# Three seven-product stretches of a fused attention and MLP kernel: fewer second products inside each set, and attention steps 17 to 23 taken one at a time

## The chip, the cores and the metric

The kernel runs on one core of a Trainium2 chip. The core has a matrix engine (TensorE, "PE" in the profile), a vector engine (VectorE, "DVE"), an activation engine (ScalarE, "ACT"), a general engine (GpSimd, "POOL") and a sync engine (SyncE, "SP") that here only issues DMA transfers. Each engine works through its own queue of instructions, and they wait for one another by semaphores. The metric is device time in microseconds (us), the median of several runs. Matrix products are written to PSUM, which this kernel uses as eight banks of 128 x 512 float32 values.

## The reference

Decayed causal linear attention, then a two-layer MLP with a tanh GELU.

```python
for b in range(nb):                      # blocks of 64 positions, for 4 batches x 8 heads, D = 64
    intra = (qb @ kb.T * Dmask) @ vb     # Dmask = lam ** (i - j) for i >= j, else 0
    inter = (qb * lam ** (i + 1)) @ kv_state
    out[b] = intra + inter
    kv_state = lam ** 64 * kv_state + (kb * lam ** (63 - j)).T @ vb
x = out as (3072 tokens, 512)
h = x @ w_in                             # 512 -> 2048
g = gelu_tanh(h)
result = g @ w_out                       # 2048 -> 512, float32, 3072 x 512
```

## The kernel before, in words

**Attention steps.** There are 24 steps: 4 batches x 3 blocks of 256 positions x 2 halves of the heads. A step `n` is made of: `prep` (`cast_q` on DVE L282, `cast_k` on ACT L295, `scale_v` on POOL L266, and for late steps a transposing DMA on SP, L303, that makes `qkT`), `scores` (16 small PE matmuls into two banks `S`, L350), `causal` (two DVE multiplies by the mask, L360, which make `PT` and free the `S` banks), the key-value products `K` and the outputs `O` of a step (PE), and `update` (DVE `t`, L503/L506, then POOL `u`, L513: the state that a later step's inter-block matmul reads). `x_out` (ACT L487) copies `O` to the MLP's input `xT`. `R(n, s)` does the scores and `K` of step n and the `O` of step s in one go with two `S` and two `OK` banks; `burst(ns, ss)` does several steps at once with up to eight banks: two `S` for each new step, two `O` and two `K`.

**MLP groups.** The twelve 256-token blocks are taken in seven groups, `groups = [[0, 1], [2], [3], [4, 5], [6, 7], [8, 9], [10, 11]]`. Groups 1 to 6 use a seven-product scheme (Winograd's form of Strassen) for the second layer, groups 4 to 6 also for the first. For a group of 512 tokens:

- `product(m, p, part)` is half (part 0 or 1) of one second-layer product: 4 matmuls of 128x128 by 128x256. The text calls one such half P. Products 1, 2, 5, 6, 3, 7, 4 follow in this order, each for p = 0 and 1, so a group has 28 halves. They accumulate in the banks `MX` (two), `MW` and `MY`. Evacuations: ACT L657 for m = 1, 5, 6, 7, 4; DVE L677 at the end of m = 2; DVE L683 at the end of m = 3.
- `sum_g` (DVE L610, out `gs`) makes the sums of GELU values that products 5, 6, 3 and 7 read, for tiles 0 to 3 and 4 to 7 separately. `sum_x` (DVE L718, out `xs`) makes four sums of `xT`; `sum_win` (DVE L151, out `ws`) makes the weight sums of the first layer.
- `seven(m, k)` is one first-layer product of set k (k = 0 to 3): also 4 matmuls of the same shape. The text calls it S(m, k). It accumulates in the banks `HX` (one for even and one for odd sets), `HY` and `HW`. Products 1, 6, 7 and 4 of a set use the same `HX` bank in turn: DVE copies U2 out after product 6 (L763), product 7 adds to the bank, DVE makes a sum of it (L770), and only then may product 4 add to it. Product 5 of the next set overwrites `HY`, so it must come after DVE's sum of product 3 (L770). GELU is ACT L767; ACT L778 and L761 are copies.

**The order.** It is written by hand. `queue_group(g, lead, per_set)` puts the pieces of a group in a list `filler`; `fill(n)` issues the next n pieces. `merge` (L798) makes a mixed stretch: it issues the four `sum_x` behind one piece, then a lead of second products left over from the group before, then the four sets of the new group's first layer with leftover P between them, as `SLOTS[per_set]` says:

```python
for m in (1, 5, 2, 6, 3, 7):
    filler.append(lambda m=m, k=k: seven(m, k))
    if m == 5 and k > 0:
        filler.append(lambda k=k: seven(4, k - 1))
    ...
    h(slots[m])          # so many leftover P after this product
```

Everything is pinned: each engine runs its instructions in the order of the program. A call such as `prep(20)` between two `fill` calls puts a DVE, an ACT and a POOL instruction, a transposing DMA and three loads on SP at that place of each queue. The tail of the program, L1093 to L1141, is what the change rewrites. It holds three mixed stretches: group 4 with the second products of group 3, group 5 with those of group 4, group 6 with those of group 5. All banks come from one pool of eight (`ps_M`).

Of the kernel before, what the change touches and what calls it, by code (L numbers as in the profile page):

```python
# [15 lines left out]
def kernel(  # L16
# [43 lines left out]
    def load_step(s, names="qkv"):  # L60
        b, r = divmod(s, 2 * NSB)
        sb, half = divmod(r, 2)
        ts = ld32.setdefault(s, [])
        for nm, src in (("q", q), ("k", k), ("v", v)):
            if nm not in names:
                continue
            t = ld.tile([P, HH, 2, D], FP32, tag=nm + "32", name=f"{nm}32_{s}")
            rows = src[b, half * HH : (half + 1) * HH, sb * SB : (sb + 1) * SB, :]
            queue = nc.scalar if (nm, s) == ("v", 0) else nc.sync
            pin(queue.dma_start(out=t[:].rearrange("p h j d -> p h (j d)"),  # L70
                                in_=rows.rearrange("h (p j) d -> p h (j d)", j=2)))
            ts.append(t)
# [97 lines left out]
    def load_ahead(s):  # L170
        if s < NSTEP:
            load_step(s)
# [72 lines left out]
    def prep(s):  # L245
        prep_qk(s)
        prep_v(s)
# [8 lines left out]
    def prep_v(s):  # L256
        scale_v(s)
        if s >= 6:
            if s + 3 == FIRST_DMA_T + 2:
                load_step(s + 3, "qk")  # L260
            else:
                load_ahead(s + 3)

    def scale_v(s):
        tv = a16p.tile([P, 2, HH, D], FP16, tag="v16", name=f"v16_{s}")
        pin(nc.gpsimd.tensor_tensor(wide(tv[:]), ld32[s][2][:], decay(dv, s), ALU.mult))  # L266
        a16[s] = a16[s] + (tv,)

    def prep_qk(s):
        cast_qk(s)  # L270
        transpose_dma(s)
# [67 lines left out]
    def half64(i):  # L339
        return slice(64 * i, 64 * i + 64)  # L340
# [3 lines left out]
    def scores(n):  # L344
        o = qkT[n]
        Sps = [ps_M.tile([P, 2, 2, P], FP32, tag="M", name=f"S{hl}") for hl in range(2)]
        for hp in range(2):
            for jk in range(2):
                for hl, c in TILES:
                    pin(nc.tensor.matmul(  # L350
                        Sps[hl][half64(c), hp, jk, :], o[half64(hl), 1, jk, hp, half64(c)],
                        o[half64(hl), 0, :, hp, half64(c)], start=True, stop=True,
                        skip_group_check=True))
        Ss[n] = Sps

    def causal(n):

        t = ptp.tile([P, 2, 2, 2, P], FP16, tag="PT", name=f"PT_{n}")
        for hl, Sps in enumerate(Ss.pop(n)):
            pin(nc.vector.tensor_tensor(  # L360
                t[:, hl].rearrange("p b c d -> p b (c d)"), Sps[:].rearrange("p b c d -> p b (c d)"),
                mask[:].unsqueeze(1).to_broadcast([P, 2, 2 * P]), ALU.mult))
        PTs[n] = t
# [51 lines left out]
    def burst(ns, ss, *mix, ahead=None):  # L415


        for i, n in enumerate(ns):
            scores(n)
            if ahead and i == 0:  # L420
                ahead()
        O = [ps_M.tile([P, 2, 2, P], FP32, tag="M", name=f"O{c}") for c in range(2)]
        seen = set()

        def start(kind, c, hl):
            new = (kind, c, hl) not in seen
            seen.add((kind, c, hl))
            return new

        qTs = [qkT.pop(s) for s in ss]  # L430
        for i, s in enumerate(ss):
            PT, tv = PTs.pop(s), a16.pop(s)[2]
            for hp in range(2):
                for jk in range(2):
                    for c, hl in TILES:
                        pin(nc.tensor.matmul(
                            O[c][half64(hl), i, hp, :], tv[half64(c), jk, 2 * hp + hl, :],
                            PT[half64(c), hl, hp, jk, :], start=start("O", c, hl), stop=False,
                            skip_group_check=True))
        if ns:  # L440
            K = [ps_M.tile([P, 2, P], FP32, tag="M", name=f"K{c}") for c in range(2)]
        for i, n in enumerate(ns):
            _, tk, tv = a16[n]
            last = (n // 2) % NSB == NSB - 1
            for jk in range(2):
                for hp in range(2):
                    for c, hl in TILES:
                        if c == 1 and last:
                            continue
                        pin(nc.tensor.matmul(  # L450
                            K[c][half64(hl), i, hp * D : hp * D + D],
                            tk[half64(c), jk, 2 * hp + hl, :], tv[half64(c), jk, 2 * hp + hl, :],
                            start=start("K", c, hl), stop=(jk == 1), skip_group_check=True))
            Kps[n] = [t[:, i] for t in K]
        for i, s in enumerate(ss):
            for c in range(2):
                if c == 0 and (s // 2) % NSB == 0:
                    continue
                u = us.pop((s, 0) if c else (s - 2, 1))
                for hp in range(2):  # L460
                    pin(nc.tensor.matmul(O[c][:, i, hp, :], u[:, hp].rearrange("p l d -> p (l d)"),
                                         qTs[i][:, 0, :, hp, half64(c)], start=False, stop=True,
                                         skip_group_check=True))
        for n in ns:
            causal(n)
        for i, s in enumerate(ss):
            x_out(s, [t[:, i].rearrange("p h t -> p (h t)") for t in O])
        sbg = ss[-1] // 2
        g, i = group_of[sbg]
        if ss[-1] % 2 == 1 and i == len(groups[g]) - 1:  # L470
            queue_group(g, *mix)
        for n in ns:
            update(n, 0)

    def x_out(s, OK, second=None):
        sbg, half = divmod(s, 2)
        g, i = group_of[sbg]
        if g not in xT:
            xT[g] = xtp.tile([P, 2, len(groups[g]), 2, SB], FP16, tag="xT", name=f"xT_{g}")
        dst = xT[g][:, half, i]  # L480
        for c in range(2):
            d = dst[:, :, c * P : (c + 1) * P].rearrange("p hp (t j) -> p hp j t", j=2)
            o = OK[c][:, 0:256].rearrange("p (hp j t) -> p hp j t", hp=2, j=2)
            if c == 1 and second is not None:
                pin(second.tensor_copy(out=d, in_=o))
            else:
                pin(nc.scalar.activation(out=d, in_=o, func=AF.Copy))  # L487
# [41 lines left out]
        return gs_kept[1:]  # L529

    SEVEN = (4, 5, 6)
    SLOTS = {5: {1: 0, 5: 1, 2: 1, 6: 1, 3: 1, 7: 1}, 4: {1: 0, 5: 1, 2: 0, 6: 1, 3: 1, 7: 1}}
    groups = [[0, 1], [2], [3], [4, 5], [6, 7], [8, 9], [10, 11]]
    group_of = {sb: (g, i) for g, sbs in enumerate(groups) for i, sb in enumerate(sbs)}
    filler = []
# [8 lines left out]
    def queue_group(g, lead=0, per_set=0):  # L544
# [253 lines left out]
        def merge(lead, per_set):  # L798
# [22 lines left out]
            unread = {1: 16, 2: 12, 4: 8, 3: 4}  # L821
            slots = SLOTS[per_set]
            for k in range(HF // 2):
# [91 lines left out]
    def fill(n):  # L915
        for _ in range(min(n, len(filler))):
            filler.pop(0)()

    def R(n, s, ahead=None, keep=False, mix=()):

        if n is not None:
            scores(n)
        if ahead:
            ahead()
        products(n, s)
        if n is not None:
            causal(n)
        if s is not None and s % 2 == 1:
            g, i = group_of[s // 2]
            if i == len(groups[g]) - 1 and g > 0:  # L930
                queue_group(g, *mix)
        if n is not None and not keep:
            update(n, 0)

    def U(n):
        update(n, 1)
# [156 lines left out]
    burst((15, 16), (13, 14), ahead=lambda: (prep_qk(17), scale_v(17)))  # L1093
    load_ahead(19)
    load_ahead(20)
    fill(1)
    U(15)
    U(16)
    fill(3)
    R(17, 15, mix=(10, 4))  # L1100
    fill(4)
    U(17)
    fill(4)
    sum_win(4, 0, nc.vector)
    prep(18)
    fill(12)
    sum_win(4, 1, nc.vector)
    prep(19)
    fill(12)
# [2 lines left out]
    prep_qk(21)  # L1112
    fill(12)

    burst((18, 19), (16, 17))
    fill(1)
    U(18)
    U(19)
    fill(3)
    R(20, 18)  # L1120
    prep_v(21)
    fill(2)
    R(None, 19, mix=(5, 4))
    U(20)
    fill(14)
    prep_qk(22)
    fill(12)
    prep_qk(23)
    fill(10)
    prep_v(22)  # L1130
    prep_v(23)
    fill(14)
    burst((21, 22), (20,))
    fill(1)
    U(21)
    U(22)
    fill(3)
    R(23, 21)
    fill(4)
    burst((), (22, 23), 3, 4)  # L1140
    fill(len(filler))  # L1141
# [28 lines left out]
```

## Time and profile before

| what | value |
|---|---|
| median of 3 runs | 204.13 us (204.03 to 205.08) |
| the profiled execution | 204.25 us |
| its span, first to last instruction | 202.5 us |
| PE busy | 191.4 us, 95% of the span |
| DVE busy | 157.8 us, 78% |
| ACT busy | 124.7 us, 62% |
| POOL busy | 70.8 us, 35% |
| DMA | 38.13 MB, mean 188 GB/s |
| granted TensorE clock | 1.000 |

The time of the profiled execution is 1.75 us over its span; that part lies outside the first and last instruction. A busy share says how long an engine was occupied over the whole span, and a matmul's own duration overlaps that of the next, so the PE's 95% does not say that only 5% could be won. Where the PE waits is read from the list of waits and from its timeline: the start of one piece to the start of the next.

The parts of the tail, from the PE timeline (us from the span's start):

| from | to | what |
|---|---|---|
| 95.25 | 98.87 | last first-layer pieces of group 3 |
| 99.64 | 100.57 | `R(17, 15)` |
| 100.57 | 104.94 | ten P of group 3, the lead |
| 104.94 | 127.23 | sets of group 4 with the other P of group 3 |
| 127.32 | 135.88 | attention 18 to 20, eleven P of group 4 |
| 135.88 | 157.72 | sets of group 5 with the other P of group 4 |
| 157.81 | 166.85 | attention 21 to 23, eleven P of group 5 |
| 166.85 | 186.57 | sets of group 6 with the other P of group 5 |
| 186.57 | 198.96 | the second layer of group 6 |

### The profile page before, as it was taken

The page shows a single profiled execution, that of the slowest core. Times are in us where ns is not written, and L with a number is a line of the kernel's source. Part 1 is how long each engine was busy: PE and PEld are TensorE (multiplying, and loading weights), DVE is VectorE, ACT ScalarE, POOL GpSimd, SP SyncE. Part 2 cuts the span into 40 slices and gives each one's busy share as a digit, 9 for nine tenths or more (in the row PEclk, how much of TensorE's full clock was granted, in tenths as well). Part 3 has the DMA queues.
Part 4 walks back from the last instruction along what each step waited for, and adds up shares of the span by engine and source line. Part 5 has one row for each costly group of instructions (what it writes and reads, how often), then busy time and mean ns, then how long its engine had stood idle before and what let it go on. Part 6 is the DMA issues. An engine that isn't in the chain of part 4 may idle for free.

```text
span 202.5 us, 6043 instructions
## 1 busy us (share of the span) xinstructions
PE 191.4 (95%) x2479; PEld 144.3 (71%) x2479; DVE 157.8 (78%) x308; ACT 124.7 (62%) x257; POOL 70.8 (35%) x85
## 2 busy tenths in 40 slices
PE   8979999999999999999896999996999999999993
PEld 2556544466888888555485888785888788888882
DVE  5987524789999898999999768999667979477620
ACT  2673878277764773867642879634877645779221
POOL 6594133457437631579462001194002040002000
PEclk9999999999999999999999999999999999999999
DMA  6999999999999999999971999320450300020205
GB/s 173 290 329 387 386 386 377 293 287 287 254 229 239 260 279 214 289 232 315 214 178 30 224 190 273 76 99 0 53 133 24 108 3 0 3 104 15 94 21 187
DMA packets 62811, 38.13 MB, mean 188 GB/s; under 512 B 18624, under 2 KB 55744, under 8 KB 62784
## 3 DMA queue, kind: packets, MB, share of 16 engines
q1 hardware_dynamic: 62240, 37.50, 74.2%
q8 instruction: 19, 0.31, 0.7%
q10 hardware_dynamic: 544, 0.26, 0.5%
q14 instruction: 8, 0.07, 0.1%
HBM read 27.26 MB, written 6.29 MB: 166 GB/s over the span
## 4 chain that ended last, share of the span: by engine, by line
PE 71%; DVE 14%; DMA 6%; SPq 4%; issue 2%; ACT 1%; POOL 0%; DVEq 0%
PE Hps L561 15%; PE MX L640 13%; PE HX L750 9%; PE MY L640 7%; PE O2ps L576 7%; PE HY L750 4%; DMA wi<-in_moe_w_in_dram 4%; SPq L70 4%; DVE gs L610 4%; DVE PT L360 3%; DVE xs L718 3%; PE Hps L847 3%; PE MW L640 3%; DMA qkT<-qk 2%; PE HW L750 2%; PE S L350 2%
## 5 line engine op out<-in xcount | busy, mean ns | idle before, releaser
L513 POOL TENSOR_TENSOR u<-t,lumask 128x256 f16<-128x256 f32 x40 | 29.6, 756 | 31.1 <-DVE t L506 23.1
L561 PE MATMUL Hps<-xT,w_in 128*128 128x256 f16 (+1 forms) x224 | 36.2, 318 | 0.0
L640 PEld LDWEIGHTS <-gs 128*128 128x128 f16 x320 | 31.2, 98 | 4.3 <-DVE gs L610 0.7
L266 POOL TENSOR_TENSOR v<-v,dv 128x512 f16<-128x512 f32 x24 | 26.9, 1127 | 16.7 <-DMA v<-in_v_dram 16.2
L360 DVE TENSOR_TENSOR PT<-S,mask 128x512 f16<-128x512 f32 x48 | 30.4, 678 | 2.4 <-PE S L350 2.4
L561 PEld LDWEIGHTS <-w_in 128*128 128x128 f16 x224 | 21.7, 98 | 12.2
L565 ACT ACTIVATE gT<-Hps 128x512 f16<-128x512 f32 x40 | 23.9, 597 | 9.2 <-PE Hps L561 8.8
L640 PEld LDWEIGHTS <-gT 128*128 128x128 f16 x240 | 23.1, 98 | 3.3 <-issue 0.6
L692 POOL TENSOR_TENSOR o<-u,q 128x512 f32<-128x512 f32 (+1 forms) x5 | 5.7, 1141 | 53.5 <-ACT u L657 53.5
L750 PEld LDWEIGHTS <-ws 128*128 128x128 f16 x192 | 18.7, 98 | 5.8 <-issue 2.4
L640 PE MATMUL MX<-w_sum,gs 128*128 128x256 f16 x160 | 22.4, 273 | 0.4 <-DVE gs L610 0.4
L295 ACT ACTIVATE qk<-k 128x512 f16<-128x512 f32 x23 | 14.4, 626 | 7.6 <-DMA k<-in_k_dram 7.3
L282 DVE TENSOR_TENSOR qk<-q,dq 128x512 f16<-128x512 f32 x23 | 17.4, 758 | 1.0 <-DMA q<-in_q_dram 1.0
L487 ACT ACTIVATE xT<-OK 128x256 f16<-128x256 f32 x32 | 12.2, 454 | 6.9 <-PE OK L408 5.3
L750 PE MATMUL HX<-xs,ws 128*128 128x256 f16 x96 | 14.4, 272 | 2.1 <-DVE w_out L763 2.1
L610 DVE TENSOR_TENSOR gs<-gT 128x1024 f16<-128x1024 f16 (+1 forms) x24 | 15.7, 665 | 0.5 <-ACT gT L565 0.5
L763 DVE COPY w_out<-HX 128x512 f32<-128x512 f32 x12 | 8.3, 688 | 9.3 <-ACT gT L767 7.0
L750 PEld LDWEIGHTS <-w_in 128*128 128x128 f16 x144 | 14.1, 98 | 2.0
L576 PE MATMUL O2ps<-w_out,gT 128*128 128x512 f16 x64 | 14.6, 379 | 0.0
L767 ACT ACTIVATE gT<-w_out 128x512 f16<-128x512 f32 x15 | 9.5, 631 | 7.2 <-DVE w_out L770 7.2
L350 PEld LDWEIGHTS <-qkT 64*64 64x64 f16 x384 | 6.0, 106 | 7.3 <-issue 3.2
L640 PE MATMUL MY<-w_out,gs 128*128 128x256 f16 x80 | 11.2, 273 | 0.0
(97 smaller groups left out, 346.7 us busy)
## 6 DMA issues: line engine op xcount, KB each, us to landing
q<-in_q_dram SPq DMA_DIRECT2D x24, 256.0 KB, 4.9
k<-in_k_dram SPq DMA_DIRECT2D x24, 256.0 KB, 5.1
v<-in_v_dram SPq DMA_DIRECT2D x23, 256.0 KB, 5.3
out_dram<-o SPq DMA_DIRECT2D x23, 256.0 KB, 3.6
wo<-in_moe_w_out_dram SPq DMA_DIRECT2D x4, 1024.0 KB, 9.5
wi<-in_moe_w_in_dram SPq DMA_DIRECT2D x4, 512.0 KB, 8.0
wi<-in_moe_w_in_dram SPq DMA_DIRECT2D x2, 1024.0 KB, 12.6
v<-in_v_dram ACTq DMA_DIRECT2D x1, 256.0 KB, 4.3
```

Source lines behind the costliest of these rows:

```text
L266: pin(nc.gpsimd.tensor_tensor(wide(tv[:]), ld32[s][2][:], decay(dv, s), ALU.mult))
L282: pin(q_eng.tensor_tensor(wide(tq), q32[:], decay(dq, s), ALU.mult))
L295: pin(nc.scalar.activation(out=wide(tk), in_=k32[:], func=AF.Copy))
L360: pin(nc.vector.tensor_tensor(t[:, hl].rearrange("p b c d -> p b (c d)"), Sps[:].rearrange("p b c d -> p b (c d)"), mask[:].unsqueeze(1).t ...
L487: pin(nc.scalar.activation(out=d, in_=o, func=AF.Copy))
L513: pin(nc.gpsimd.tensor_tensor(u[:], state[half][:].unsqueeze(2).to_broadcast([P, 2, 2, D]), lumask[:, 2 * half : 2 * half + 2, :].unsqueez ...
L561: pin(nc.tensor.matmul(by_block(Hps[:, i, :]), w_in16[:, c, f * P : (f + 1) * P], x(c), start=(c == 0), stop=(c == NC - 1)))
L565: pin(nc.scalar.activation(out=dst, in_=Hps[:], func=AF.Gelu_apprx_tanh))
L576: pin(nc.tensor.matmul(O2[tau][0][:], gT[:, f % HF, f // HF, tau * P : (tau + 1) * P], w_out16[:, f, :], start=(n == 0), stop=(n == NF - 1)))
L610: pin(nc.vector.tensor_tensor(g_rows(m, i), g_rows(a, i), g_rows(b, i), op))
L640: pin(nc.tensor.matmul(dst, lhsT, rhs, start=(opens and i == 0), stop=(closes and i == HF - 1), skip_group_check=True))
L750: pin(nc.tensor.matmul(dst[:, i, :], w_in_block(a, slice(c, c + 1), slice(f * P, f * P + P))[:, 0], x_block(b, slice(c, c + 1))[:, 0], sta ...
```

## The change

`SLOTS` gets a third entry: three leftover P per set, where the one after product 7 is gone. Groups 4 and 5 use it in place of the entry with four. Before the sets begin, more P are issued: 14 of 28 instead of 10 for group 4 and 11 for group 5; for group 6 it is 12 instead of 11. Four of group 4's come ahead of `R(17, 15)`. The bursts of steps 18/19 and 21/22 become single `R` calls with P between them; the outputs of 18 and 19 are taken together in one call of `burst` without new steps. The calls of `prep`, `prep_qk`, `prep_v`, `sum_win` and `U` move with respect to the pieces. `U(22)` and `U(23)` only forget a bank: those steps are the last block of a batch. No instruction is added or removed but for the change of bank layout that `R` and `burst` have.

```diff
-    SLOTS = {5: {1: 0, 5: 1, 2: 1, 6: 1, 3: 1, 7: 1}, 4: {1: 0, 5: 1, 2: 0, 6: 1, 3: 1, 7: 1}}
+    SLOTS = {5: {1: 0, 5: 1, 2: 1, 6: 1, 3: 1, 7: 1}, 4: {1: 0, 5: 1, 2: 0, 6: 1, 3: 1, 7: 1},
+             3: {1: 0, 5: 1, 2: 0, 6: 1, 3: 1, 7: 0}}
...
     burst((15, 16), (13, 14), ahead=lambda: (prep_qk(17), scale_v(17)))
     load_ahead(19)
     load_ahead(20)
-    fill(1)
     U(15)
     U(16)
+    fill(8)
+    R(17, 15, mix=(10, 3))
     fill(3)
-    R(17, 15, mix=(10, 4))
-    fill(4)
     U(17)
+    fill(3)
+    prep(18)
     fill(4)
     sum_win(4, 0, nc.vector)
-    prep(18)
-    fill(12)
+    fill(6)
     sum_win(4, 1, nc.vector)
     prep(19)
     fill(12)
     prep(20)
     fill(12)
     prep_qk(21)
     fill(12)
 
-    burst((18, 19), (16, 17))
+    R(18, 16)
     fill(1)
+    prep_v(21)
     U(18)
+    fill(2)
+    R(19, 17)
+    fill(1)
     U(19)
     fill(3)
-    R(20, 18)
-    prep_v(21)
-    fill(2)
-    R(None, 19, mix=(5, 4))
+    burst((), (18, 19), 7, 3)
+    fill(3)
+    R(20, None)
+    fill(1)
     U(20)
-    fill(14)
+    fill(11)
     prep_qk(22)
     fill(12)
     prep_qk(23)
     fill(10)
     prep_v(22)
     prep_v(23)
-    fill(14)
-    burst((21, 22), (20,))
+    fill(13)
+    R(21, None)
     fill(1)
     U(21)
-    U(22)
+    fill(1)
+    R(22, 20)
     fill(3)
     R(23, 21)
-    fill(4)
+    U(22)
+    U(23)
+    fill(3)
     burst((), (22, 23), 3, 4)
     fill(len(filler))
```

## The prediction

> **What bounds the kernel now.** First the page: PE is busy 95% of the span and DVE 78%, so PE sets the time where it doesn't wait. Then the list of PE's waits from 90 us on (us in total, times, longest):
>
> ```profile
> PE HX L750 <- DVE w_out L763: 2.1, 2, 1.3
> PE HY L750 <- DVE ws L151: 1.0, 1, 1.0
> PE S L350 <- DMA qkT<-qk: 0.8, 1, 0.8
> PE MX L640 <- DVE gs L610: 0.4, 1, 0.4
> ```
>
> All but one name DVE, all in the first set of a stretch or ahead of it. The PE timeline gives a price: in a mixed stretch each piece (a P or an S) starts 0.437 us after the last (119.30, 119.74, 120.17). Group 4 has 56 pieces from 100.57 to 127.23: 24.4 of work in 26.66, so 2.2 of waits, nearly all before 110.52. Then the DVE timeline of that place (start, us):
>
> ```profile
> 102.29 0.83 DVE L718 TENSOR_TENSOR xs<-xT 128x512 f16<-128x512 f16 x1
> 103.23 1.08 DVE L718 TENSOR_TENSOR xs<-xT,xs 128x512 f16<-128x512 f16 x1
> 104.23 1.26 DVE L718 TENSOR_TENSOR xs<-xT 128x512 f16<-128x512 f16 x1
> 105.41 0.41 DVE L718 TENSOR_TENSOR xs<-xT,xs 128x512 f16<-128x512 f16 x1
> ...
> 107.99 0.68 DVE L151 TENSOR_TENSOR ws<-w_in,ws 128x1024 f16<-128x1024 f16 x1
> 108.59 0.68 DVE L282 TENSOR_TENSOR qk<-q,dq 128x512 f16<-128x512 f32 x1
> 109.19 0.68 DVE L770 TENSOR_TENSOR w_out<-HW,w_out 128x512 f32<-128x512 f32 x1
> 109.79 0.67 DVE L763 COPY w_out<-HX 128x512 f32<-128x512 f32 x1
> ...
> 111.59 0.67 DVE L770 TENSOR_TENSOR w_in<-HX,w_in 128x512 f32<-128x512 f32 x1
> ```
>
> DVE has no gap here: one instruction each 0.60 us, the `xs` sums up to 1.2 while POOL scales v (0.42 without, at 167.38). PE follows 0.73 after the DVE start that it waits for: 107.99 to 108.72 (S3 of set 0), 109.79 to 110.52 (S7), 111.59 to 112.32 (S4). So the start of each stretch is a DVE queue, and the rest is PE. In the rest one loop is tight: S7, DVE's L770, S4 on the same bank. These lines are from DVE and PE:
>
> ```profile
> 116.01 0.69 DVE L770 TENSOR_TENSOR w_in<-HX,w_in 128x512 f32<-128x512 f32 x1
> ```
> ```profile
> 115.37 0.60 PE L750 MATMUL HX<-xs,ws 128*128 128x256 f16 x4
> 117.12 0.60 PE L750 MATMUL HX<-xs,w_in 128*128 128x256 f16 x4
> ```
>
> L770 starts 0.64 after S7, so S4 is ready 0.64 + 0.73 = 1.37 after it; with four pieces from S7 to S4 it is asked for at 1.75. 0.38 is to spare.
>
> **The Trainium skill.** In "TensorE: Matmul & The Clock Gate", section "Architectural detail": DVE and ACT are strict FIFO; the trace agrees (S3 waits for L151, which stands behind sums it doesn't need). In "GPSIMD Engine Reference", section "Specifications": POOL shares SBUF interfaces with DVE, in contention with DVE instructions with two SBUF inputs; the trace agrees (0.34 to 0.42 against about 1.0), while L770 and L677, with one PSUM input, stay at 0.60. In "PSUM — Partial Sum Buffer", section "Specifications (TRN2)": eight banks per partition; the code's bursts use all eight, and the trace has PE waiting for banks there (0.17 and 0.21 behind the mask products, at 129.38 and 159.68).
>
> **The change part by part.** No arithmetic is added: the same pieces, DVE, ACT and POOL instructions, DMAs. Only waits can change. I walk each stretch with the durations above, in program order, and compare at equal work (each piece more that is already done is worth 0.437).
>
> *Group 4, lead.* Removed: four P go before `R(17, 15)`, which starts at 98.74 + 4 x 0.437 + 0.09 = 100.58, so the transpose that landed by 99.64 is covered (0.8 gained). R takes 0.93 as before, P2 starts at 101.51, and ten lead pieces end at 105.87. Unhindered, S3 of set 0 would start at 108.49 and S7 at 109.37. DVE: mask products at 101.05 (0.47 after the scores as before), `t` to 102.63, four `xs` beside POOL's u17, v18 and v19 (as slow as before) to 106.4, L677 to 107.0, `gs` to 107.8, q18 to 108.4, `gs` 109.0, `ws` 109.0 to 109.6: S3 at 109.73, 1.24 late. L770 of S2 to 110.2, U2 copy at 110.2: S7 at 110.93, 0.32 late. Now the moved calls bite: `sum_win(4, 1)` and q19 stood after S7's sum and now stand before S3's. `ws` to 111.4, q19 to 112.0, S3's L770 at 112.0: S5 of set 1 at 112.73, asked for at 111.80 (0.93 late). S7's L770 at 112.6: S4 at 113.33 (0.16). Before, S4 of set 0 was at 112.32; three pieces more are done, so the even point is 113.63: 0.3 gained so far, though the lead is longer by 1.75.
>
> *Three per set.* The P after S7 is gone, so S4 is asked for 3 x 0.437 = 1.31 after S7 and ready at 1.37: 0.06 lost in each such set, if DVE is free. In set 1 of group 4 it isn't. From S6 at 114.64: U2 copy 115.34, S3's L770 116.2 to 116.8, L683 (the second product 3 of group 3 ends here now) to 117.4, q20 to 118.0 (`prep(20)` now stands before S7, it stood behind S1), S7's L770 at 118.0. S4 is ready at 118.73 and asked for at 117.70: 1.03 lost. Set 2 loses 0.06. DVE has gaps of over a microsecond before and after, but its queue can't use them. Group 4: 0.3 - 1.03 - 0.06 = 0.8 lost.
>
> *Attention 18 to 20, group 5.* T is the end of the last S4 of group 4. The banks need no burst of eight any more. DVE finishes group 4's `gs` at T+1.7 (before: 1.4), because the last S4 and its GELU now come last. Mask products of 18 to 2.9, two `t` to 3.5, mask products of 19 to 4.7, `t` to 5.3. POOL: u18 3.3, v21 3.9 to 5.0 (1.1), u18 again, u19 5.6 to 6.2. v21 now stands ahead of u19. PE: R(18, 16) to 1.02, three P, R(19, 17) to 3.35, four P to 5.1, O of 18 and 19; the last two matmuls need u19: 6.33, 0.67 lost. Then seven P and R(20), with S1 of set 0 at 10.0. DVE meanwhile waits for the last P2: L677 at 7.1, four `xs` to 9.06 (0.34 each: POOL is idle), `gs` to 9.66 (P6 waits for it, 0.23 lost), mask products of 20 to 10.9, then `t`, `gs`, `t`, `gs` (slow beside u20 and v22) to 13.45, L770, and the U2 copy at 14.05: S7 at 14.78, asked for at 13.72 (1.06 lost). S3's L770, q22 (which now stands before S7's sum, beside POOL's v23), S7's L770 at 16.05: S4 at 16.78. Before, S4 of set 0 was at 143.24, T+16.01, with two pieces fewer: even point 16.88. Gained 0.1. In set 1 L683 stands before S7's L770 again, without a q: S4 ready 21.58, asked for 21.14 (0.44 lost); set 2 0.06. What the old stretch lost there was 0.1. Group 5: 0.3 lost.
>
> *Attention 21 to 23, group 6.* From T' (end of the last S4): P, R(21), two P, R(22, 20), whose second bank waits for the mask product of 21 (0.7), three P, R(23, 21), three P, O of 22 and 23 behind u23 at 7.75. S1 at 9.3 to 9.5. DVE is behind: the mask products and `t` of 21 to 23 take it to 6.9, then L677, `gs`, four `xs` behind `x_out`, two `gs`, L770, U2 copy at 12.3 to 12.5: S7 at 13.03 to 13.23. Before: 170.35 = T'+12.63 with one piece less, even point 13.07. Between nothing and 0.16 lost, taken as 0.1. Four per set stay here, and the second layer of group 6 behind it is unchanged.
>
> *DMAs.* The transposes of 18 to 23 and loads 21 to 23 follow their casts on SP; each is needed over 5 us later (a transpose lands in 3.8), so I cost them at nothing; one that came late would stop an R for what it is late, and 0.8 was such a case.
>
> Sum: 0.8 + 0.3 + 0.1 = 1.2 us on the profiled execution's 204.25 (span 202.5 to 203.7): 205.45. The runs' median is 0.12 lower, so 205.3.
>
> What the old trace doesn't show: how slow a `gs` or q cast beside POOL is at the new places (q took 0.60 at 108.59 and 1.02 from 93.26, beside POOL's u). From 1.2 less than taken, if POOL's work lies beside DVE's PSUM reads, to 1.0 more, if every sum and cast of a lead is slow; I take slow exactly where POOL's queue overlaps by the sums above. And which bank a tile gets: with single R calls and `MX` held between them it can cost from 0 (a free bank) to about 1.1 more (a bank that waits for both mask products at 0.6 each). I take a free bank except at R(22), where none is.
>
> **The rivals.** A change within 0.5%, which is about what a measurement of this kernel can tell from none: the gains of the longer leads and the queue in set 1 cancel. It takes 1.2 us less of DVE queue in all; the 1.03 of set 1 is the surest loss, the 0.93 at S5 the one most easily smaller. 204.2.
>
> Faster: PE's longer lead wins. If DVE works off group 4's lead without POOL's drag (four `xs` at 0.34 to 0.42, 1.4 instead of 3.8), the waits at S3, S7, S5 and S4 (1.24, 0.32, 0.93, 0.16 = 2.65) vanish and the time is 205.3 - 2.65 = 202.7. It decides from about 1.2 us of relief on. Against it: POOL's order u17, v18, v19 isn't changed, and u17 still follows `t`.
>
> Slower than forecast: banks. Each R takes four, `MX` two, and R before it still holds some until its `t`; if R(19), R(22) and R(23) each wait for one that DVE frees late, 1.1 more: 206.4.
>
> The change does what it says: each engine runs the program's order in the trace, so the order can't fail to take effect.
>
> **How the numbers follow.** Forecast 205.3, chance 0.45, own range 204.6 to 206.0; banks 0.13; no change 0.25; faster 0.17. The threshold of 0.5% is 205.15, inside the forecast's own range, so 0.08 of its 0.45 counts as within. Slower by over 0.5%: 0.37 + 0.13 = 0.50; within: 0.25 + 0.08 = 0.33; faster: 0.17. The range from 203.0 to 206.6 leaves out about 0.1 on the fast side and less on the other.
>
> **What would show it.** Right: no wait of S17 for its transpose; S4 of set 1 in group 4 waits about 1 us for L770, with L683 and L282 ahead of it on DVE; S5 of set 1 waits for L770; O of 18 and 19 waits for u; the three tail stretches together are longer by about 1.2. Wrong: S7 of group 4 at its unhindered place, `xs` sums at 0.4, or DVE idle when S4 waits.

## The result and the profile after

The changed kernel takes 205.67 us (median of 20 runs, 205.12 to 206.12) against 204.65 us of the kernel before, measured beside it (20 runs). The ratio is 1.0042, 95% interval 1.0024 to 1.0060: 0.42% slower, which is clear of no change but just short of the 0.5% that the prediction drew as its line; the interval reaches over that line, so the runs don't settle on which side the change lies. The forecast was 1.2 us more (on a base of 204.13, the median of three runs); by the medians 1.0 was measured. Of the three cases that the prediction weighed, the likeliest (slower by over 0.5%) did not come by this ratio; "within 0.5%" did.

The profiled execution of the changed kernel took 206.03 us (span 204.2). The source has one line more above the sums, so L763, L770 and L683 of before are now L764, L771 and L684. The list of PE's waits from 90 us on:

```profile
PE HX L751 <- DVE w_in L771: 2.5, 4, 1.0
PE HY L751 <- DVE ws L151: 1.6, 1, 1.6
PE HY L751 <- DVE w_out L771: 0.8, 1, 0.8
PE HX L751 <- DVE w_out L764: 0.3, 1, 0.3
PE MX L641 <- DVE gs L611: 0.2, 1, 0.2
```

The wait for the transpose is gone and the wait at the U2 copy has shrunk from 2.1 to 0.3. In their place PE waits 3.3 us for L771, DVE's sums that free a bank inside a set, which before didn't appear in the list at all. The two largest waits for these sums are S4 of set 0 in group 5 (0.96) and S4 of set 1 in group 4 (0.89), where the prediction put its surest loss. PE's and DVE's timelines at the second (start, duration):

```profile
116.97 0.60 PE L751 MATMUL HX<-xs,ws 128*128 128x256 f16 x4
117.40 0.60 PE L751 MATMUL HX<-xT,w_in 128*128 128x256 f16 x4
117.84 0.60 PE L751 MATMUL HY<-xs,ws 128*128 128x256 f16 x4
119.33 0.60 PE L751 MATMUL HX<-xs,w_in 128*128 128x256 f16 x4 [0.89 <-DVE w_in L771]
```
```profile
115.93 0.69 DVE L764 COPY w_out<-HX 128x512 f32<-128x512 f32 x1 [2.06 <-PE HX L751]
116.79 0.69 DVE L771 TENSOR_TENSOR w_out<-HY,w_out 128x512 f32<-128x512 f32 x1 [0.17 <-PE HY L751]
117.40 0.68 DVE L684 TENSOR_TENSOR o<-MY,u 128x512 f32<-128x512 f32 x1
118.00 0.68 DVE L282 TENSOR_TENSOR qk<-q,dq 128x512 f16<-128x512 f32 x1
118.59 0.68 DVE L771 TENSOR_TENSOR w_in<-HX,w_in 128x512 f32<-128x512 f32 x1
```

S7 starts at 116.97 and its sum could have started 0.64 later, at 117.61. It starts at 118.59, because L684 and the cast of q20 stand ahead of it. PE, two pieces further on, stops from 118.28 to 119.33. The first line shows DVE idle for 2.06 us just before: there was room, at another place of the queue.

### The profile page after: what moved, and what is told of

The parts are those of the page before. It is cut to its first block, busy times and chain, and to the rows that moved or that the text cites. A ratio compares the mean times of both kernels' runs of the same rounds, so it can differ in the third digit from the quotient of the medians.

```text
span 204.2 us, 6043 instructions
## 1 busy us (share of the span) xinstructions
PE 192.7 (94%) x2479; PEld 144.2 (71%) x2479; DVE 155.6 (76%) x308; ACT 125.0 (61%) x257; POOL 71.9 (35%) x85
## 4 chain that ended last, share of the span: by engine, by line
PE 74%; DVE 13%; SPq 4%; DMA 4%; issue 2%; ACT 1%; DVEq 0%
PE Hps L562 17%; PE MX L641 14%; PE HX L751 8%; PE O2ps L577 7%; PE MY L641 6%; DMA wi<-in_moe_w_in_dram 4%; SPq L70 4%; PE HY L751 4%; PE MW L641 3%; PE S L350 3%; PE Hps L848 3%; DVE gs L611 2%; DVE w_out L771 2%; PE HW L751 2%; PE OK L408 2%
## 5 line engine op out<-in xcount | busy, mean ns | idle before, releaser
L513 POOL TENSOR_TENSOR u<-t,lumask 128x256 f16<-128x256 f32 x40 | 31.2, 793 | 33.6 <-DVE t L506 25.6
L266 POOL TENSOR_TENSOR v<-v,dv 128x512 f16<-128x512 f32 x24 | 26.3, 1101 | 18.7 <-DMA v<-in_v_dram 16.0
L282 DVE TENSOR_TENSOR qk<-q,dq 128x512 f16<-128x512 f32 x23 | 18.7, 813 | 1.8 <-DMA q<-in_q_dram 1.6
L487 ACT ACTIVATE xT<-OK 128x256 f16<-128x256 f32 x34 | 13.0, 452 | 8.6 <-PE OK L408 8.2
L764 DVE COPY w_out<-HX 128x512 f32<-128x512 f32 x12 | 8.2, 687 | 12.9 <-PE HX L751 9.3
L506 DVE SCALAR_TENSOR_TENSOR t<-t,lamu,OK 128x64 f32<-128x64 f32 x52 | 11.9, 273 | 1.2 <-issue 0.5
```

Source lines behind the costliest of these rows:

```text
L282: pin(q_eng.tensor_tensor(wide(tq), q32[:], decay(dq, s), ALU.mult))
L513: pin(nc.gpsimd.tensor_tensor(u[:], state[half][:].unsqueeze(2).to_broadcast([P, 2, 2, D]), lumask[:, 2 * half : 2 * half + 2, :].unsqueez ...
```

## The experiments

The ratios are to the kernel before, with 95% intervals. The changed kernel is 1.0042.

### One half of the change at a time

`a_new` takes the new code up to the end of group 4's stretch and the old code from attention 18 on; `bc_new` is the other way round.

```diff
 # a_new: the tail from here on as before
     fill(12)
+    burst((18, 19), (16, 17))
-    R(18, 16)
 ...
```

> Only the part up to the end of group 4's mixed stretch is changed (R(17, 15) after four P, lead of 14, three P per set, moved prep and sum_win calls); attention 18 to 23 and groups 5 and 6 are as before. DVE-queue theory: this part holds nearly all of the loss, 1.2 to 1.4 us slower than before in the profile, with S3, S5 and S4 of set 1 waiting 1.6, 0.8 and 0.9 us. Rival (splitting the bursts costs the time, the moved calls little): within 0.4 us of before.

Measured: 1.0035 (1.0019 to 1.0052), 204.92 us. That is 0.7 us slower, not 1.2 to 1.4. S5 (0.8) and S4 of set 1 (0.9) wait as said; S3 waits 1.1 instead of 1.6, which is most of the difference (what sets it is read in the last experiment).

> Only the part from R(18, 16) on is changed (single attention calls, lead of 14 and three per set in group 5); group 4's stretch is as before. DVE-queue theory: 0.0 to 0.4 us slower than before, since what the longer lead gains at S7 is lost at S4 of sets 0 and 1. Rival (splitting the bursts costs the time): 1 us slower or more, with PE waits at the R calls.

Measured: 1.0030 (1.0012 to 1.0049), 204.80 us. No R call waits for a bank in its list; S4 of sets 0 and 1 of group 5 waits 1.0 and 0.3. So about 0.6 us are lost in this part (the interval goes from 0.2 to 1.0), by its middle more than the 0.0 to 0.4 expected. Its profile also has a longer wait for the transpose (1.2 instead of 0.8), in code that isn't changed there, so the part's share isn't known closer than some tenths. Each half is slower by itself and neither can be called the cause alone. Together they give 0.65%, above the 0.42% of the whole; the intervals leave room for both. The rival on split bursts has no wait to show for it.

### Calls put back behind the sums

```diff
 # q_later
-    fill(12)
+    fill(14)
     prep(20)
-    fill(12)
+    fill(10)
```

> The changed kernel with one call moved: prep(20) stands two pieces later, behind S1 of set 2, where it was before. DVE-queue theory: the wait of S4 of set 1 in group 4 falls from 0.9 us to about 0.3 (L683 still stands ahead of the sum), so 0.6 us faster than the changed kernel. Rival (three P per set leaves S4 too close to S7 whatever DVE does): the wait stays at about 0.9 and the time is the same.

Measured: 1.0026 (1.0007 to 1.0046), 204.75 us. The wait of S4 falls from 0.89 to 0.28 in the profile, as the queue theory had it. Against the kernel before, the ratio falls by 0.16% (about 0.3 us), less than the 0.6 of the profile; the two intervals overlap, so the size isn't settled by the times. The lowest run of the changed kernel, 205.12, and that of this one, 204.63, are 0.5 apart (the kernel before had 204.03 and 204.00 beside them).

```diff
 # ws_later
-    fill(6)
+    fill(9)
     sum_win(4, 1, nc.vector)
     prep(19)
-    fill(12)
+    fill(9)
```

> The changed kernel with sum_win(4, 1) and prep(19) three pieces later, behind S7 of set 0, so behind both of its sums on DVE. DVE-queue theory: the waits of S5 (0.8 us) and S4 (0.16) of set 0 go, 0.8 to 1.0 us faster than the changed kernel. Rival (DVE is short of time in the whole stretch): the wait shows up again at S7 or S4 of set 1 and the time is the same.

Measured: 1.0002 (0.9985 to 1.0019), 204.38 us, 0.4% or 0.8 us less than the changed kernel. S5's wait is gone from the list and nothing took its place: S4 of set 1 still waits 0.89, neither more nor less. Two calls three pieces later, `sum_win(4, 1)` and `prep(19)`, are worth nearly all of what the change lost.

```diff
 # both_later: both of these, and q22 in group 5
-    fill(11)
+    fill(12)
     prep_qk(22)
-    fill(12)
+    fill(11)
```

> The changed kernel with three calls put back behind the sums of their set: sum_win(4, 1) with prep(19) behind S7 of set 0 of group 4, prep(20) behind S1 of set 2, prep_qk(22) behind S7 of set 0 of group 5. DVE-queue theory: the waits at S5 (0.8), S4 of set 1 (0.9 to 0.3) in group 4 and S4 of set 0 (0.96 to about 0.3) in group 5 go, 1.8 us faster than the changed kernel, so about 0.8 us faster than before. Rival (the single removals overlap, since DVE is short of time as a whole): no more than 1.0 us faster than the changed kernel, level with before.

Measured: 0.9922 (0.9901 to 0.9943), 202.86 us: 1.2% (about 2.4 us) under the changed kernel, more than the 1.8 expected, and 0.8% faster than before. The removals don't eat one another, and the rival (no more than 1.0 us) falls. What the third move, that of q22, is worth by itself was not measured. What PE waits for is now:

```profile
PE HY L751 <- DVE ws L151: 1.0, 1, 1.0
PE HX L751 <- DVE w_in L771: 0.9, 3, 0.3
PE HX L751 <- DVE w_out L764: 0.3, 1, 0.3
PE MX L641 <- DVE gs L611: 0.2, 1, 0.2
```

### POOL beside the sums of the lead

`v_early` is `both_later` with v18 and v19 scaled ahead of `R(17, 15)`, so ahead of u17 on POOL. `tuned` takes q18 out of the lead as well.

```diff
     fill(8)
+    a16_late(18)      # scale_v into a v tile that prep_qk picks up later
+    a16_late(19)
     R(17, 15, mix=(10, 3))
 ...
-    prep(18)
+    load_ahead(21)
 # v_early: prep_qk(18) stays here; tuned: it goes behind S7 of set 0, with prep_qk(19)
```

> As both_later, and the lead of group 4 freed: POOL scales v of 18 and 19 ahead of R(17, 15), and q of 18 is cast behind S7 of set 0. POOL-contention theory: the four xs sums ahead of group 4 take 1.4 to 2.0 us instead of 3.5, q18 is out of the lead, and the wait of S3 of set 0 (1.1 to 1.6) and that of S7 go: another 1.1 to 1.5 us, about 2 us faster than before. Rival (xs is slow for another reason, or v19 comes too late from memory and slows xs again): the S3 wait falls only by the 0.6 of q18.

Measured: 0.9847 (0.9824 to 0.9871), 201.24 us. That is 1.5% faster than before (3.2 us less than the 204.43 measured beside it), and the best version of the study. S3 waits for nothing.

> As both_later, and only the POOL part of tuned: v of 18 and 19 scaled ahead of R(17, 15); q18 stays in group 4's lead. POOL-contention theory: the four xs sums take 1.7 to 2.0 us from start to end instead of 3.4 to 3.6, S3 of set 0 no longer waits (1.0 before), 0.8 to 1.1 us faster than both_later. Rival (q18's 0.6 in the lead is what made S3 wait, and POOL's work only changes places): 0.4 us or less faster than both_later.

Measured: 0.9863 (0.9835 to 0.9891), 201.77 us, 0.6% or 1.2 us less than `both_later`, and S3 waits for nothing here either. So with POOL's work out of the way S3 is free although q18 still stands in the lead; q18 was not moved by itself, and its further 0.16% in `tuned` lies within the intervals. DVE's `xs` sums in `both_later`, then in `v_early`:

```profile
102.79 0.42 DVE L719 TENSOR_TENSOR xs<-xT 128x512 f16<-128x512 f16 x1
103.31 0.65 DVE L719 TENSOR_TENSOR xs<-xT,xs 128x512 f16<-128x512 f16 x1
103.88 1.26 DVE L719 TENSOR_TENSOR xs<-xT 128x512 f16<-128x512 f16 x1
105.06 1.26 DVE L719 TENSOR_TENSOR xs<-xT,xs 128x512 f16<-128x512 f16 x1
```
```profile
103.43 0.41 DVE L728 TENSOR_TENSOR xs<-xT 128x512 f16<-128x512 f16 x1
103.95 0.65 DVE L728 TENSOR_TENSOR xs<-xT,xs 128x512 f16<-128x512 f16 x1
104.52 0.41 DVE L728 TENSOR_TENSOR xs<-xT 128x512 f16<-128x512 f16 x1
104.86 0.41 DVE L728 TENSOR_TENSOR xs<-xT,xs 128x512 f16<-128x512 f16 x1
```

From the first start to the last end, 3.5 us become 1.8. They begin 0.64 later, since v18 now meets a `gs` sum ahead of them (1.42 us at 100.51, against 0.69 in `both_later`), so their end comes 1.05 earlier (105.27 instead of 106.32).

### The old leads with a lighter queue

`old_clean` is the kernel before, four P per set and short leads, with v18 and v19 early, q18 behind the sums of set 0, and v21 and v22 ahead of the updates of 18 and 19.

```diff
     fill(3)
+    a16_late(18)
+    a16_late(19)
     R(17, 15, mix=(10, 4))
 ...
     sum_win(4, 0, nc.vector)
-    prep(18)
     fill(12)
     sum_win(4, 1, nc.vector)
-    prep(19)
+    prep_qk(18)
+    prep_qk(19)
 ...
-    burst((18, 19), (16, 17))
+    burst((18, 19), (16, 17), late=lambda: (prep_v(21), a16_late(22)))
 ...
-    prep_v(21)      # and, further down, prep_v(22)
```

> The kernel before, its leads and four P per set kept, with only the DVE and POOL queues in front of the sets lightened: v of 18 and 19 ahead of R(17, 15), q18 cast behind the sums of set 0, v of 21 and 22 ahead of the updates of 18 and 19. DVE-queue theory: the waits of S3 and S7 in group 4 (1.75 together) and of S7 in group 5 (1.3 and 0.4) mostly go, 1.5 to 2.5 us faster than before. Rival (the lead of ten or eleven P is too short whatever the queue holds): no more than 0.5 us faster than before.

Measured: 0.9907 (0.9886 to 0.9927), 202.44 us, 1.9 us faster than before, as the queue theory had it. In the lists S3 waits 0.6 instead of 1.0, and S7 of the two groups together 0.8 instead of 2.1. So most of what PE lost at the start of a stretch came from the DVE and POOL queues, not from the length of the lead; the longer lead is worth something on top (`tuned` is 0.6% lower), though `tuned` also has the transpose covered.

### Where the missing P stands

```diff
-             3: {1: 0, 5: 1, 2: 0, 6: 1, 3: 1, 7: 0}}
+             3: {1: 0, 5: 0, 2: 0, 6: 1, 3: 1, 7: 1}}
```

> The changed kernel with the P of each set of three taken from after product 5 and put after product 7, so four pieces from S7 to S4 again and three from S1 to S2. Tight-loop theory: S4 of sets 1 and 2 waits 0.44 less each (0.9 to 0.45 and 0.3 to 0), S4 of set 0 in group 5 0.5; S2 waits under 0.1 each for ACT's copy; 0.8 to 1.2 us faster than the changed kernel. Rival (any loop of three pieces is as bad, the loss moves to S2): within 0.3 us of the changed kernel.

Measured: 0.9992 (0.9970 to 1.0013), 203.99 us, 0.5% or 1.0 us under the changed kernel, as the tight-loop theory has it. But the run doesn't tell it apart from the queue: with the pieces counted anew, `prep(20)` fell behind S7 of set 1 and `sum_win(4, 1)` behind the sum of S3, which alone accounts for much of it. Hence the same edit on `tuned`, where the calls keep their places.

> As tuned, with the P of each set of three taken from after product 5 and put after product 7; every moved call stands behind the same S as in tuned, so that L683 is the only DVE instruction that changes its place against the sums. Tight-loop theory: S4 of set 1 no longer waits 0.29 in groups 4 and 5, nor 0.06 in the other sets; S2 waits under 0.1 each for ACT's copy of HX; 0.4 to 1.0 us faster than tuned. Rival (the loss moves to S2 behind ACT): within 0.3 us of tuned.

Measured: 0.9866 (0.9829 to 0.9902), 201.84 us: not faster than `tuned`; the ratio is 0.2% (0.4 us) higher, within the intervals. The S4 waits of sets 1 and 2 are gone and S2 waits for nothing, so the loops behave as said. But taking the P after product 5 also takes one from the stretch ahead of S7 in set 0, and the loss reappears there:

```profile
PE HY L760 <- DVE ws L151: 0.7, 1, 0.7
PE HX L760 <- DVE w_out L773: 0.7, 1, 0.7
```

The expectation had left out that the first set has the same slots. Part of the 0.7 at S3 is a `ws` sum of 1.52 us beside v20 on POOL in this profile.

### The changed kernel once more

> The changed kernel itself, profiled once more, since its runs fall into two heaps (205.1 to 205.6 and 205.8 to 206.1 us) and its first profile is from the upper one. If the heaps come from where POOL's scaling of v20 falls, which starts when its transfer lands: in a run of the lower heap v20 starts before 107.0, q18 or gs beside it takes 1.0 us or less instead of 1.5, and S3 of set 0 waits 1.1 instead of 1.6. If not, S3 waits 1.6 in a run of the lower heap too.

Measured: 205.42 us in one profiled execution, span 203.6. POOL's L266 in the first profile, then in this one:

```profile
103.73 2.40 POOL L266 TENSOR_TENSOR v<-v,dv 128x512 f16<-128x512 f32 x2
107.25 1.26 POOL L266 TENSOR_TENSOR v<-v,dv 128x512 f16<-128x512 f32 x1 [1.13 <-DMA v<-in_v_dram]
```
```profile
103.71 3.58 POOL L266 TENSOR_TENSOR v<-v,dv 128x512 f16<-128x512 f32 x3
```

And DVE's cast of q18, in the same order:

```profile
107.53 1.53 DVE L282 TENSOR_TENSOR qk<-q,dq 128x512 f16<-128x512 f32 x1
```
```profile
107.77 0.68 DVE L282 TENSOR_TENSOR qk<-q,dq 128x512 f16<-128x512 f32 x1
```

In the first, v20's transfer landed late, its scaling met the cast of q18, and S3 waited 1.61. Here v20 followed v19 at once and S3 waited 1.03. The two executions are 0.61 us apart, and 0.6 is what differs at S3. Ten of the twenty runs lie in each heap, so the median of 205.67 stands between them. Two profiles show the mechanism; that it explains every run of the upper heap is only argued.

## Why the prediction was right, and where it wasn't

**Group 4, lead.** Right, nearly to the step. In the first profile `R(17, 15)` began at 100.63 (said 100.58), P2 at 101.56 (101.51), and S3 in the second profile (`again`) at 109.71 (109.73). S5 lost 0.93 (0.93) and S4 of set 0 lost 0.15 (0.16). Off in one term: in the first profile S3 was at 110.32, since q18, taken at 0.60, took 1.53.

**Three per set, set 1.** Right. S4 lost 1.05 (1.03), in set 2 0.07 (0.06). `q_later` shows that the cast is its larger part. Group 4 as a whole: from 98.74 to 127.23 before, from 98.79 to 128.63 after, so 1.35 lost instead of 0.8; in the second profile the next R begins 0.60 earlier, at 128.12 instead of 128.72, and the stretch (98.75 to 128.03) lost 0.79, the 0.8 that was said.

**Group 5.** The sum was 0.3 and 0.05 was measured (from 128.63 to 159.17, 30.54, against 30.49). The step that failed is the wait for u19, "0.67 lost": the last matmuls of steps 18 and 19 didn't wait. With T for the end of group 4's last S4 (128.63), DVE was done with group 4's `gs` at T+1.2, not T+1.7, and v21 took 1.04 and the `u` 0.6, so u19 was ready when PE came. Later DVE reached the U2 copy of set 0 at T+13.3, not T+14.05: the two `gs` sums and two `t` ahead of it, taken as slow beside POOL, took 2.0 instead of 2.55. So S7 lost 0.44, not 1.06. S4 of set 0 lost 1.1 rather than 0.7 and S4 of set 1 0.46 (0.44): the place was right, and the sum of S7 and S4 came out only a little smaller.

**Group 6.** Said 0.1, measured 0.33 (from 159.17 to 188.35, against 157.72 to 186.57). S7 began 12.96 after the last S4 of group 5, a little ahead of what was said (13.03 to 13.23). The bank for R(22) cost 0.2, not 0.7. What was missed is the last S4, which lost 0.51. PE before, then PE and DVE of the changed kernel:

```profile
184.76 0.60 PE L750 MATMUL HX<-xs,ws 128*128 128x256 f16 x4
185.19 1.04 PE L640 MATMUL MX<-w_sum,gT 128*128 128x256 f16 x8
186.14 0.60 PE L750 MATMUL HX<-xs,w_in 128*128 128x256 f16 x4
```
```profile
186.54 0.60 PE L751 MATMUL HX<-xs,ws 128*128 128x256 f16 x4
186.97 0.60 PE L641 MATMUL MX<-w_sum,gT 128*128 128x256 f16 x4
187.92 0.60 PE L751 MATMUL HX<-xs,w_in 128*128 128x256 f16 x4 [0.34 <-DVE w_in L771]
```
```profile
187.18 0.69 DVE L771 TENSOR_TENSOR w_in<-HX,w_in 128x512 f32<-128x512 f32 x1
```

With eleven P in the lead 17 of the 28 were left, and two stood between the last S7 and S4. With twelve, the four sets use up the other 16, and one stands there. DVE isn't late: its sum begins 0.64 after S7, as ever, and S4 follows 0.74 later, so it is ready 1.38 after S7 and asked for at 0.87. The prediction had this loop at 1.37, but took group 6's sets as unchanged ("Four per set stay here"). The runs that keep two P there (`a_new`, `old_clean`) don't have this wait; all others show 0.34 or 0.35 at that S4, `tuned` too.

1.35 + 0.05 + 0.33, and 0.05 already at 98.79, make the 1.78 between the two profiled executions (204.25 and 206.03). In the second profile (205.42) the three parts lost 0.79, 0.04 and 0.34, together 1.17, against the 1.2 that was said. That the sum fits so well is luck in part: group 5 came out 0.26 better than said and group 6 0.24 worse. By medians the change costs 1.0.

**The rivals.** Banks: no wait for a bank of more than about 0.2 us in the attention steps. No change: within the drawn line, but not for the reason given; the queue in set 1 was there at full size. Faster: it asked for about 1.2 us of relief on DVE, and `v_early` gave about that by taking POOL from the `xs` sums: their end came 1.05 earlier and the time fell by 1.2. The mechanism was right; nothing in the change itself moved POOL's work, as was held against it.

## What to carry to other kernels

Where one engine's queue is strictly in order, a prefetch cast costs its place, not its time: put it where the engine is about to be idle, behind the instruction that a bank waits for, and the same work is free. Taking cover out of a loop (here one P between S7 and S4) leaves no slack for anything that later lands in that queue, so check what the new piece count does to the order of every helper call, and to the last set, which gets only the pieces that are left. Before making a lead longer, see why the engine behind it is slow: here scaling two v tiles earlier on POOL was worth 1.2 us on top of the longer lead, which by itself had not taken S3's wait away.

## What the runs showed of the hardware

A DVE instruction with two operands in SBUF (where this kernel keeps the tiles that aren't in PSUM) that starts while a POOL tensor operation runs does not just slow down in proportion: in these traces it ends about when it would if it had begun at the end of that POOL instruction. The cast of q18 started at 107.53 beside v20, which ended at 108.51: 0.98 left and 0.55 of its own, and 1.53 was measured. The `gs` sum in group 6:

```profile
183.70 1.64 DVE L611 TENSOR_TENSOR gs<-gs,gT 128x1024 f16<-128x1024 f16 x1
```
```profile
183.27 1.52 POOL L693 TENSOR_TENSOR o<-u,q 128x512 f32<-128x512 f32 x1 [16.64 <-ACT u L658]
```

POOL was done at 184.79, 1.09 after the sum began; 0.55 more gives 1.64 (at this place it cost PE nothing: the U2 copy behind it began 0.71 after S6, as in the kernel before). The `xs` sums of 1.26 fit too: about 0.96 left of v18 and 0.3. The same subtraction in all traces of this study, from 95 us on, wherever single instructions can be told apart, covers rests of POOL from 0.17 to 1.19: duration less rest is 0.53 to 0.56 for the `gs` and `ws` sums and the cast, which take 0.67 to 0.69 alone, and 0.27 to 0.29 for `xs` (0.41 alone). It goes the other way as well: a v scaling that starts during such a DVE instruction takes the rest of that and about 0.9 (1.04 alone), which gives the 1.1 to 1.5 seen; `u` takes the rest and about 0.47 (0.61 alone). DVE instructions with an operand in PSUM keep their duration beside POOL: in the changed kernel L764 took 0.67 at 141.90 and L771 0.69 at 142.71, both while v was scaled. That it is a lock for the length of an instruction is a reading of these cases; no run measured it by itself.
